# Attention queries of two heads in row halves of the array, denominators on GpSimd, numerators in column halves

## The chip, the core and the metric

The program runs on one core of a Trainium2 chip. The metric is the time of one execution on the device in microseconds (us); a run is compared by its median. The engines are TensorE (PE, matrix products; PEld is its weight load), VectorE (DVE), ScalarE (ACT), GpSimd (POOL) and SyncE (SP, which here issues the DMA transfers). Matrix results land in PSUM, eight banks of 2 KB per partition; everything else lies in SBUF.

## What is computed

A linear attention, then a mixture of four experts, then a gated network; all in 32-bit floating point.

```python
def phi(x):
    proj = np.einsum('bhsd,df->bhsf', x, w_phi)
    proj = proj - np.max(np.abs(proj), axis=-1, keepdims=True)
    return np.concatenate([np.exp(proj), np.exp(-proj)], axis=-1)
q_p, k_p = (phi(q), phi(k))                     # (4, 8, 576, 256)
kv = np.einsum('bhsf,bhsd->bhfd', k_p, v)
z = np.sum(k_p, axis=2)
num = np.einsum('bhsf,bhfd->bhsd', q_p, kv)
den = np.einsum('bhsf,bhf->bhs', q_p, z)[..., None] + 1e-06
x = num / den                                   # as 2304 tokens x 512
...
for e in range(4):
    out += p[:, e:e + 1] * (np.maximum(x @ w1[e], 0.0) @ w2[e])
...
y = (((out @ v1) * (out @ v2)) @ w3) @ w_out
```

## The kernel before

**Recording and order.** The program text does not issue instructions: `op` (L130) and `dma` (L341) record operations with an engine, a guess of their duration, and what they read, write and fill. `Prog.run` (L281) plays the record through a list scheduler with those guesses, once by priority and twice more by due times, and then issues everything in the order that came out. So each engine's queue holds the order that the planner chose, and a changed guess, buffer count or priority moves instructions everywhere. Priorities come from `pg.base`, `KLEAD` and `AHEAD` (how far ahead of the expert work an attention pair is put). In the first 110 us the planner also issues filler products (`spin`, L467, tile `fill_z`) into the gaps that it foresees on TensorE.

**Attention.** Batches and heads are taken as 16 pairs of heads (`p` 0 to 15). `k_side` (L506) projects the keys of both heads, each with its 64 rows in one row half of the array (L540), takes the exponentials, and sums features times values into one PSUM bank `kvp` in column halves (L553); column 64 of the values' tile is a one, so that z falls out as one more column. ScalarE copies the result to `KV`, for pairs 6 to 15 (`SPLIT`) rounded to the one-pass 32-bit format with VectorE's remainder beside it (L591, L594). `q_side` (L605) then works head by head (`h`), half a sequence at a time (`s`, 288 columns): a load of q that brings the 64 rows twice, a rounded copy in the upper rows and the remainder in the lower (L613, L614), two products `Pq` (L623, L624), a copy to SBUF `Ps` (L628), the largest absolute value over the 128 partitions by GpSimd `M` (L631), the subtraction on VectorE (L634), two exponentials into `Eq` (L639). For pairs 6 to 15 `Eq` is split again into a rounded tile and a remainder (L645, L647). The product `num` (L655) has 128 output rows: 64 of the numerator and 64 copies of the denominator; it takes two products in full precision (each stands as two records in the trace), or six of the rounded format for the split pairs. A copy `xq` (L660), a small DMA of the denominator's row to `d9`, a reciprocal, a DMA out and back that spreads it over 64 partitions (`rb`), and one multiplication per head (L680) give the attention output `xr`.

**Experts.** Expert weights come in 16 chunks `c`. Token group 0 (768 tokens) is computed with plain products for the first `KA` = 8 chunks, since these can run while later attention pairs are still at work: per chunk and half group two times twelve products `up` (L800 by `plain_up`), a ReLU on ScalarE and its remainder on VectorE (L855, L857), and three times six products `dn` (L869) that VectorE adds up in `acc` (L890). One half group of one chunk is called a turn below; there are 2 x `KA` = 16. All later chunks and groups use a Strassen scheme (`upa`, `upb`, `upc`, seven times six products in place of eight, by `strassen_up`), with weights prepared by GpSimd (L391, L419). It starts when all of attention is done (`phase_c`) and holds the rest of the program, with `fold` (w3 times w_out, tile `psw`) and the gated network.

**PSUM.** In the attention stage pool `aps` has five banks (`kvp` 1, `kp` 2, `qp` 1, `num` 1) and pool `mma` three, from which `up` and `dn` take turns. Afterwards `mma` keeps its three and `mmb` takes the other five.

Of the kernel before, what the change touches and what calls it, by code (L numbers as in the profile page):

```python
# [308 lines left out]
def fused_kernel(ctx, tc, qT, kT, vt, w_phi, probs, w1, w2, v1, v2, w3T, w_out, out):  # L309
# [196 lines left out]
    def k_side(p):  # L506
# [72 lines left out]
        halves = [
            (lambda t: t()[:, :, 0:4:3], lambda: kvp()[:, :, :, 0:64]),  # L580
            (lambda t: t()[:, :, 1:3], lambda: kvp()[:, :, :, 64:65].to_broadcast([128, 2, 2, 64])),
        ]
        if p not in SPLIT:
            KV = [V("at", [128, 2, 4, 64], F32, "KV0", 2, f"KV{p}")]
            for part, src in halves:
                op(ACT, act(256, False), lambda part=part, src=src: nc.scalar.copy(out=part(KV[0]), in_=src()),
                   reads=[kvp], fills=KV)
        else:
            KV = [V("at", [128, 2, 4, 64], F32R, f"KV{i}", 2 - i, f"KV{i}_{p}") for i in range(2)]
            for part, src in halves:  # L590
                op(ACT, act(256, False), lambda part=part, src=src: nc.scalar.copy(out=part(KV[0]), in_=src()),  # L591
                   reads=[kvp], fills=KV[:1])
            for part, src in halves:
                op(DVE, dve(256), lambda part=part, src=src: nc.vector.tensor_tensor(  # L594
                    out=part(KV[1]), in0=src(), in1=part(KV[0]).bitcast(F32), op=ALU.subtract
                ), reads=[kvp, KV[0]], fills=KV[1:])
# [8 lines left out]
    def q_side(p, KV):  # L605
        b, pr = divmod(p, 4)
        xq = V("at", [128, 2, S], F32, "xq", 2, f"xq{p}")
        d9 = V("at", [128, 2 * S // 128], F32, "d9", 3, f"d9_{p}")
        rd = V("dram", [1, 2 * S], F32, f"rd{p}", 1, f"rd{p}")
        for h in range(2):  # L610
            qr = qr0 if p == h == 0 else load_q(p, h)
            q2 = V("at", [128, S], F32R, "q2", 2, f"q2{p}_{h}")
            op(ACT, act(S), lambda qr=qr, q2=q2: nc.scalar.copy(out=q2(), in_=qr()), reads=[qr], writes=[q2])  # L613
            op(DVE, 786, lambda qr=qr, q2=q2: nc.vector.tensor_tensor(  # L614
                out=q2()[64:128], in0=qr()[64:128], in1=q2()[64:128].bitcast(F32), op=ALU.subtract
            ), reads=[qr], writes=[q2], port=True)
            for s in range(2):
                nm = f"{p}_{h}{s}"
                sl = slice(s * HS, (s + 1) * HS)
                P = V("aps", [128, HS], F32, "num" if p < ALONE and s else "qp", 1, f"Pq{nm}")  # L620

                def proj(P=P, q2=q2, sl=sl):
                    nc.tensor.matmul(P(), wst(), q2()[:, sl], start=True, stop=False)  # L623
                    nc.tensor.matmul(P(), wlo(), q2()[:, sl], start=False, stop=True)  # L624
# [512 lines left out]
```

## Time and profile before

| | |
|---|---|
| median of 3 runs | 1261.15 us (1260.68 to 1261.97) |
| the profiled execution | 1263.01 us, of which the traced span is 1261.2 us |
| busy share of the span | PE 99%, PEld 89%, DVE 74%, ACT 50%, POOL 43% |
| chain that ended last | PE 90%, DVE 5%, DMA 2%, ACT 2% |
| granted TensorE clock | full in nearly every slice |
| first `up` product | 84.7 us after the start |
| first `upa` product (Strassen) | 294.9 us after the start |

The busy time of TensorE is the union of pipelined products, so that a stretch at 100% may still hold waits; what a product takes is read from the distance between starts. The three stretches that the two starts in the table cut out are called the early stage (0 to 84.7), the mixed stage (84.7 to 294.9: attention pairs between plain turns) and the expert stage (the rest).

### The profile page before, as it was taken

The numbers are of one execution on the slowest core, as the hardware profiler recorded it, in microseconds if no ns is written. First come the engines' busy times: TensorE is split into PE (matmuls) and PEld (weight loads), VectorE is DVE, ScalarE is ACT, GpSimd is POOL, SyncE is SP. The second block draws the span as 40 slices with busy tenths as digits, with TensorE's granted clock in tenths as the row PEclk, the third lists the DMA queues.
The fourth block names the chain that finished last, engine by engine and source line by source line (L and its number), as shares of the span: only waits on it lengthen the run. The fifth ranks groups of instructions, "written<-read, shape, count | busy, mean of one in ns | idle before, by whom it ended". The sixth has DMA issues, their size and how long they took to land.

```text
span 1261.2 us, 19437 instructions
## 1 busy us (share of the span) xinstructions
PE 1247.6 (99%) x7449; PEld 1125.8 (89%) x7449; DVE 934.2 (74%) x1446; ACT 628.4 (50%) x1231; POOL 546.9 (43%) x374
## 2 busy tenths in 40 slices
PE   8999999999999999999999999999999999999998
PEld 7779988899999999988889888898899999999997
DVE  6698999979787885587687785698998647634454
ACT  7888888745433333344434343454445545443321
POOL 3432323316333333054544455466676677435220
PEclk9999999999999999999999999999999999999999
DMA  5654454222333321023535432143332212211002
GB/s 173 176 183 130 146 176 140 79 88 84 109 110 109 109 92 43 19 87 121 163 121 176 145 131 83 52 134 115 123 100 78 79 51 84 84 34 51 1 1 100
DMA packets 53197, 128.55 MB, mean 102 GB/s; under 512 B 10352, under 2 KB 14832, under 8 KB 53104
## 3 DMA queue, kind: packets, MB, share of 16 engines
q1 hardware_dynamic: 53104, 127.32, 31.5%
q8 instruction: 58, 0.95, 0.3%
q14 instruction: 35, 0.29, 0.1%
HBM read 109.84 MB, written 17.38 MB: 101 GB/s over the span
## 4 chain that ended last, share of the span: by engine, by line
PE 90%; DVE 5%; DMA 2%; ACT 2%; issue 1%; SPq 0%; DVEq 0%; ACTq 0%
PE dn L869 38%; PE upa L800 13%; PE upb L800 7%; PE up L800 4%; PE psw L940 3%; PE upc L800 3%; PE num L655 3%; PE kvp L553 1%; PE upa_4a L800 1%; PE upa_3b L800 1%; PE upa_3a L800 1%; PE upa_5b L800 1%; PE upa_5a L800 1%; PE upa_4b L800 1%; DVE xr L680 1%
## 5 line engine op out<-in xcount | busy, mean ns | idle before, releaser
L869 PE MATMUL dn<-w_b,h 128*128 128x512 f32 x1728 | 423.7, 391 | 0.0
L869 PEld LDWEIGHTS dn<-w_b,h 128*128 128x128 f32 x1728 | 320.7, 188 | 57.5 <-DVE acc L890 0.3
L391 POOL TENSOR_TENSOR w_a<-raw_a,w_a 128x768 fp32r<-128x768 f32 (+2 forms) x80 | 165.5, 2069 | 227.5 <-ACT w_a L389 202.1
L890 DVE SCALAR_TENSOR_TENSOR acc<-dn,pn,acc 128x512 f32<-128x512 f32 x270 | 200.3, 745 | 54.5 <-PE dn L869 52.6
L391 POOL TENSOR_TENSOR w_b<-raw_b,w_b 128x1024 fp32r<-128x1024 f32 x48 | 122.7, 2555 | 228.3 <-ACT w_b L389 223.2
L631 POOL PARTITION_ALL_REDUCE M<-Ps x64 | 86.4, 1361 | 169.5 <-ACT Ps L628 135.0
L800 PE MATMUL upa<-x_T,w_a 128*128 128x384 f32 x720 | 146.2, 337 | 0.0
L800 PEld LDWEIGHTS upa<-x_T,w_a 128*128 128x128 f32 x720 | 128.5, 187 | 7.2 <-ACT s L823 0.7
L823 ACT COPY s<-upa 128x384 f32<-128x384 f32 x120 | 57.5, 479 | 121.2 <-PE upa L800 120.9
L419 POOL TENSOR_TENSOR raw_a<-raw_a 128x256 f32<-128x256 f32 x128 | 109.8, 858 | 18.3 <-DVE acc L890 6.2
L389 ACT CAST w_b<-raw_b 128x1024 fp32r<-128x1024 f32 x61 | 64.3, 1054 | 103.4 <-PE dn L869 62.7
L869 PE MATMUL dn<-w_b,g 128*128 128x512 f32 x432 | 105.7, 390 | 0.0
L389 ACT CAST w_a<-raw_a 128x1024 fp32r<-128x1024 f32 (+2 forms) x93 | 84.5, 908 | 41.1 <-PE upb L800 16.6
L869 PEld LDWEIGHTS dn<-w_b,g 128*128 128x128 f32 x432 | 80.5, 188 | 13.7
L800 PE MATMUL up<-x_B,w_a 128*128 128x384 f32 x384 | 72.2, 338 | 0.0
L655 PE MATMUL num<-Eq,KV 128*128 128x288 f32 x336 | 67.4, 334 | 3.3 <-ACT xq L660 1.8
L800 PEld LDWEIGHTS up<-x_B,w_a 128*128 128x128 f32 x384 | 66.2, 188 | 1.0
L655 PEld LDWEIGHTS num<-Eq,KV 128*128 128x128 f32 x336 | 51.8, 188 | 10.9 <-ACT xq L660 3.8
L639 ACT ACTIVATE Eq<-Ps 128x288 f32<-128x288 f32 x128 | 51.5, 458 | 15.7 <-DVE Ps L634 15.4
L920 DVE TENSOR_TENSOR oacc<-dn,oacc 128x512 f32<-128x512 f32 x54 | 36.8, 687 | 19.0 <-PE dn L869 18.8
L800 PE MATMUL upa<-x_B,w_a 128*128 128x384 f32 x240 | 49.1, 339 | 0.0
L800 PE MATMUL upb<-x_B,w_a 128*128 128x384 f32 x240 | 49.0, 339 | 0.0
(213 smaller groups left out, 2241.7 us busy)
## 6 DMA issues: line engine op xcount, KB each, us to landing
raw_a<-w SPq DMA_DIRECT2D x37, 512.0 KB, 3.4
raw_b<-w SPq DMA_DIRECT2D x37, 512.0 KB, 3.7
qr<-qT SPq DMA_DIRECT2D x32, 288.0 KB, 3.2
near<-w3T SPq DMA_DIRECT2D x16, 512.0 KB, 4.2
raw_b<-near_wo SPq DMA_DIRECT2D x16, 512.0 KB, 4.3
near<-v SPq DMA_DIRECT2D x16, 512.0 KB, 4.8
vx<-vt SPq DMA_DIRECT2D x16, 330.0 KB, 4.3
kr<-kT SPq DMA_DIRECT2D x15, 320.0 KB, 3.9
```

What stands on the lines that cost most here:

```text
L389: lambda: op(ACT, act(n, sbuf), lambda: nc.scalar.copy(out=hi(), in_=raw[1]()), reads=[*raw[:1], *raw[2:]], fills=[w], after=after),
L391: lambda: op(eng, ns, lambda: e.tensor_tensor(out=lo(), in0=raw[1](), in1=hi().bitcast(F32), op=ALU.subtract), reads=[raw[0], w, *raw[2:]] ...
L419: ops.append(lambda to=to, a=a, b=b, how=how: op(POOL, gp(256), lambda: nc.gpsimd.tensor_tensor(out=raw()[:, to], in0=raw()[:, a], in1=raw ...
L631: op(POOL, 1300, lambda M=M, Ps=Ps: nc.gpsimd.partition_all_reduce(M(), Ps(), channels=128, reduce_op=bass_isa.ReduceOp.absmax), reads=[Ps ...
L639: op(ACT, act(HS), lambda a=a, E=E, Ps=Ps: nc.scalar.activation(out=E()[:, a], in_=Ps(), func=AF.Exp, scale=1.0 - 2 * a), reads=[Ps], fill ...
L655: nc.tensor.matmul(num(), KV[i]()[:, a, 2 * h:2 * h + 2].rearrange("p c d -> p (c d)"), EE[j]()[:, a], start=n == 0, stop=n == len(parts) - 1)
L800: nc.tensor.matmul(ps(), w()[:, a, i, kk * 128:kk * 128 + 128], x()[:, j, kk], start=first and n == 0, stop=last and n == total - 1, skip_ ...
L823: op(ACT, act(TB, False), lambda: nc.scalar.copy(out=t(), in_=ps()), reads=[ps], writes=[t], after=start["C"])
L869: nc.tensor.matmul(ps(), hs[fc]()[:, x, t * 128:(t + 1) * 128], w()[:, fc * 2:fc * 2 + 2, y], start=fc == 0 and n == 0, stop=fc == 1 and n ...
L890: op(DVE, dve(DM) + 61, lambda a=a, ps=ps, share=share: nc.vector.scalar_tensor_tensor(out=a(), in0=ps(), scalar=share(), in1=a(), op0=ALU ...
L920: op(DVE, dve(DM), lambda a=a, ps=ps: nc.vector.tensor_tensor(out=a(), in0=ps(), in1=a(), op=ALU.add), reads=[ps], writes=[a])
L940: nc.tensor.matmul(ps(), wa[v]()[:, k, a, f * 128:f * 128 + 128], wb[v]()[:, 2 * k:2 * k + 2, b], start=g == 0 and k == 0 and n == 0, stop ...
```

## The change

- q of both heads of a pair is loaded once, one head in each row half. `Pq` is then six products (three for each head) on row halves, the two heads' one after the other; pair 0 (`EXACT`) takes q and w_phi in full precision without a split.
- `KV` is one copy in full precision for all pairs; `SPLIT` and the split of `Eq` are gone. Pairs 0 to 4 (below `ALONE` = 5) multiply in full precision with 128 output rows as before. From pair 5 on, the numerators of both heads are formed in column halves of one product tile, and the denominators elsewhere: VectorE weights `Eq` by z (`W`, two instructions), GpSimd adds over the partitions.
- `xq` of pairs 5 to 15 holds both heads on 128 partitions, so that one multiplication gives `xr`.
- `KA` is 7 in place of 8 and `EB` 4 in place of 5: 14 turns, and one Strassen visit more for group 0; two folds move before the last visit of the first kind. `AHEAD` is scaled down.
- Pool `mma` has two banks in place of three (`qp` has two in place of one); after attention a pool `mmx` adds the third again.

```diff
-KA = 8
-EB = 5
-SPLIT = (6, 7, 8, 9, 10, 11, 12, 13, 14, 15)
+KA = 7
+EB = 4
+ALONE = 5
+MORE = 3
+EXACT = (0,)
+QBUFS = 2
-COLUMNS = 130.0
-ALONE = 3
+COLUMNS = 120.0
-AHEAD = (0.05, 0.6, 1.5, 2.4, 2.9, 4.5, 5.5, 6.5, 7.5, 8.5, 9.5, 10.5)
+AHEAD = (0.04, 0.48, 1.2, 1.92, 2.32, 3.6, 4.4, 5.2, 6.0, 6.2, 7.0, 7.8)
-NEAR = (24, 8, 0)
+NEAR = (40 - 2 * (16 - KA), 8, 0)
...
-    pools["mma"] = ec(tc.tile_pool(name="mma", bufs=3, space=PSUM))
+    pools["mma"] = ec(tc.tile_pool(name="mma", bufs=2, space=PSUM))
...
+        KV = V("at", [128, 2, 2, 66], F32, "KV", 2, f"KV{p}")
+        op(ACT, act(264, False), lambda: nc.scalar.copy(out=KV(), in_=kvp()), reads=[kvp], writes=[KV])
         return KV
...
+        qr = load_q(p) if p else qr0
+        rows = [slice(h * 64, h * 64 + 64) for h in range(2)]
+        if p in EXACT:
+            terms = [(lambda: wphi(), lambda: qr())]
+            used = [qr, wphi]
+        else:
+            q2 = V("at", [128, 2, S], F32R, "q2", QBUFS, f"q2{p}")
+            op(ACT, act(S), lambda: nc.scalar.copy(out=q2()[:, 0], in_=qr()), reads=[qr], writes=[q2])
+            op(DVE, dve(S), lambda: nc.vector.tensor_tensor(
+                out=q2()[:, 1], in0=qr(), in1=q2()[:, 0].bitcast(F32), op=ALU.subtract
             ), reads=[qr], writes=[q2], port=True)
+            terms = [(lambda i=i: (wst, wlo)[i](), lambda j=j: q2()[:, j]) for i, j in PASSES]
+            used = [q2, wst, wlo]
+        for s in range(2):
+            sl = slice(s * HS, (s + 1) * HS)
+            Pq = [V("aps", [128, HS], F32, "qp", 2, f"Pq{p}_{h}{s}") for h in range(2)]
+
+            def proj(Pq=Pq, sl=sl):
+                for x, (a, q) in enumerate(terms):
+                    for h in range(2):
+                        nc.tensor.matmul(Pq[h](), a()[rows[h]], q()[rows[h], sl], start=x == 0, stop=x == len(terms) - 1,
+                                         skip_group_check=True)
+
+            op(PE, 915 if len(terms) == 1 else 600, proj, reads=used, writes=Pq)
...
+                W = V("at", [128, HS], F32, "W", 2, f"W{nm}")
+                op(DVE, 280, lambda W=W, E=E, h=h: nc.vector.tensor_scalar(
+                    out=W(), in0=E()[:, 0], scalar1=KV()[:, 0, h, ones[h]:ones[h] + 1], scalar2=None, op0=ALU.mult
+                ), reads=[E, KV], writes=[W], port=True)
+                op(DVE, dve(HS) + 61, lambda W=W, E=E, h=h: nc.vector.scalar_tensor_tensor(
+                    out=W(), in0=E()[:, 1], scalar=KV()[:, 1, h, ones[h]:ones[h] + 1], in1=W(), op0=ALU.mult, op1=ALU.add
+                ), reads=[E, KV], writes=[W], port=True)
+                op(POOL, 1300, lambda W=W, h=h, sl=sl: nc.gpsimd.partition_all_reduce(
+                    D()[:, sl] if h else xq()[:, 1, sl], W(), channels=128, reduce_op=bass_isa.ReduceOp.add
+                ), reads=[W], fills=[D if h else xq], port=600)
+            if p >= ALONE:
+                num = V("aps", [128, HS], F32, "num", 1, f"num{p}_{s}")
+
+                def product(num=num, Es=Es):
+                    for a in range(2):
+                        for h, E in enumerate(Es):
+                            nc.tensor.matmul(
+                                num()[h * 64:h * 64 + 64], KV()[:, a, h, 2 * h:2 * h + 64], E()[:, a], start=a == 0, stop=a == 1,
+                                skip_group_check=True,
+                            )
+
+                op(PE, 1390, product, reads=[KV, *Es], writes=[num])
+                op(ACT, act(HS, False), lambda num=num, sl=sl: nc.scalar.copy(out=xq()[:, 0, sl], in_=num()),
+                   reads=[num], fills=[xq])
...
-            for h in range(2):
+            for h in range(2) if p < ALONE else (0,):
+                half = slice(h * 64, h * 64 + 64) if p < ALONE else slice(0, 128)
...
+    folds = deque(("fold", n, (), None) for n in range(16))
+    for c in range(KA, NE * NQ):
+        if c >= NE * NQ - (8 - KA):
+            visits += [folds.popleft(), folds.popleft()]
+        visits.append(("expert", c, (1, 0), None))
...
+        if late:
+            banks[0] += 1
+            pool = ("mma", "mma", "mmx")[banks[0] % 3]
```

The order moves with it. On TensorE, around the first turn of the second half group (tile names: `num_HS` is head and half, `Pq_HS` likewise, `x_B` the tokens of a plain turn), before:

```order
L800 MATMUL up_10_2233<-x_B_1444,w_a_1936 128x384 x6
L800 MATMUL up_10_2233<-x_B_1882,w_a_1936 128x384 x6
L655 MATMUL num_00_2256<-Eq_9_00_2121,KV_9_2211 128x288
L655 MATMUL num_00_2256<-Eq_9_00_2161,KV_9_2211 128x288
L655 MATMUL num_00_2256<-Eq_9_00_2121,KV_9_2226 128x288
L655 MATMUL num_00_2256<-Eq_9_00_2121,KV_9_2211 128x288
L655 MATMUL num_00_2256<-Eq_9_00_2161,KV_9_2211 128x288
L655 MATMUL num_00_2256<-Eq_9_00_2121,KV_9_2226 128x288
L623 MATMUL Pq_00_2268<-q_0_2087,wst 128x288
L624 MATMUL Pq_00_2268<-q_0_2087,wlo 128x288
L800 MATMUL up_11_2272<-x_B_1444,w_a_1936 128x384 x6
```

and in the change:

```order
L828 MATMUL up_10_2060<-x_B_1473,w_a_1793 128x384 x6
L828 MATMUL up_10_2060<-x_B_1852,w_a_1793 128x384 x6
L670 MATMUL num_1_2087<-Eq_01_2044,KV_2011 64x288
L670 MATMUL num_1_2087<-Eq_11_2058,KV_2011 64x288
L670 MATMUL num_1_2087<-Eq_01_2044,KV_2011 64x288
L670 MATMUL num_1_2087<-Eq_11_2058,KV_2011 64x288
L619 MATMUL Pq_01_2101<-q_1736,wst 128x288
L619 MATMUL Pq_11_2103<-q_1736,wst 128x288
L619 MATMUL Pq_01_2101<-q_1736,wst 128x288
L619 MATMUL Pq_11_2103<-q_1736,wst 128x288
L619 MATMUL Pq_01_2101<-q_1736,wlo 128x288
L619 MATMUL Pq_11_2103<-q_1736,wlo 128x288
```

Where six full-array products of one head and one half and two of `Pq` stood, there are now four in column halves for both heads and six in row halves for both heads; the array goes from full to column halves to row halves to full, where it stayed full before. Over the whole order the array's division changes 98 times before and 155 times in the change, 52 and 96 of them from the first `up` to the first `upa`.

On GpSimd, at pairs 6 and 7, before (`M` is the largest absolute value):

```order
L631 ISA M_00_1261<-Ps_00_1256 128x288
L631 ISA M_01_1322<-Ps_01_1318 128x288
L631 ISA M_10_1394<-Ps_10_1388 128x288
L631 ISA M_11_1438<-Ps_11_1434 128x288
L631 ISA M_00_1601<-Ps_00_1596 128x288
```

and in the change:

```order
L630 ISA M_00_1423<-Ps_00_1412 128x288
L630 ISA M_10_1443<-Ps_10_1421 128x288
L661 ISA xq_1408<-W_00_1433 128x288
L661 ISA D_1491<-W_10_1441 128x288
L630 ISA M_01_1536<-Ps_01_1518 128x288
L630 ISA M_11_1560<-Ps_11_1532 128x288
L661 ISA xq_1408<-W_01_1530 128x288
L661 ISA D_1491<-W_11_1534 128x288
L630 ISA M_00_1629<-Ps_00_1622 128x288
```

Two sums over `W` now stand between the maxima of one half and those of the next, so that a next maximum waits behind two sums, and these wait for VectorE's `W`.

## Rows read from the trace of the kernel before

**Rows 1.** The page: busy time, share of the span and instructions by engine.

```profile
PE 1247.6 (99%) x7449; PEld 1125.8 (89%) x7449; DVE 934.2 (74%) x1446; ACT 628.4 (50%) x1231; POOL 546.9 (43%) x374
```

**Rows 2.** Windows of the stages: length, busy us by engine, clock, DMA.

```profile
0.00:84.70 84.70, 77.69 (x872) 62.55 (x872) 60.73 (x120) 67.54 (x178) 33.64 (x31) 1.00 0.61 181
84.70:294.90 210.20, 207.31 (x1708) 187.56 (x1707) 193.18 (x334) 160.43 (x362) 63.17 (x46) 1.00 0.39 122
...
294.90:1261.20 966.30, 962.62 (x4874) 875.65 (x4872) 680.31 (x995) 400.41 (x691) 450.05 (x298) 1.00 0.28 91
```

**Rows 3.** Timeline, TensorE, mixed stage: start us, length us, records.

```profile
226.73 0.96 PE L655 MATMUL num<-Eq,KV 128*128 128x288 f32 x6
227.53 0.30 PE L623 MATMUL Pq<-q,wst 128*128 128x288 f32 x1
...
227.79 1.55 PE L869 MATMUL dn<-w_b,h 128*128 128x512 f32 x6
```

**Rows 4.** Timeline, TensorE, early stage: `num` in full precision.

```profile
20.11 2.21 PE L655 MATMUL num<-Eq,KV 128*128 128x288 f32 x8
```

**Rows 5.** The same, later, four records.

```profile
71.13 1.24 PE L655 MATMUL num<-Eq,KV 128*128 128x288 f32 x4
```

**Rows 6.** Timeline, TensorE, mixed stage: column halves, row halves and their neighbours.

```profile
233.67 0.96 PE L655 MATMUL num<-Eq,KV 128*128 128x288 f32 x6
234.56 1.15 PE L553 MATMUL kvp<-vx,E 128*64 128x66 f32 x32
235.64 0.40 PE L623 MATMUL Pq<-q,wst 128*128 128x288 f32 x1
...
238.26 1.16 PE L540 MATMUL P<-wphi,kr 64*128 64x128 f32 x16
239.35 2.35 PE L800 MATMUL up<-x_B,w_a 128*128 128x384 f32 x12
241.54 0.42 PE L655 MATMUL num<-Eq,KV 128*128 128x288 f32 x2
```

**Rows 7.** Groups on VectorE, mixed stage: busy us, mean ns, idle before.

```profile
L647 DVE TENSOR_TENSOR Eq<-Eq,Eq 128x576 fp32r<-128x576 f32 x40 | 30.9, 773 | 1.4 <-ACT Eq L645 1.3
L890 DVE SCALAR_TENSOR_TENSOR acc<-dn,pn,acc 128x512 f32<-128x512 f32 x36 | 26.5, 741 | 3.0 <-PE dn L869 2.9
...
L614 DVE TENSOR_TENSOR q<-qr,q 64x576 fp32r<-64x576 f32 x18 | 14.0, 779 | 1.5 <-ACT q L613 1.0
L391 DVE TENSOR_TENSOR w_a<-raw_a,w_a 128x1024 fp32r<-128x1024 f32 x11 | 14.0, 1269 | 0.8 <-ACT w_a L389 0.7
...
L680 DVE TENSOR_TENSOR xr<-xq,rb 64x384 f32<-64x384 f32 x16 | 9.8, 615 | 3.7 <-DMA rb<-rd 3.5
L594 DVE TENSOR_TENSOR KV<-kvp,KV 128x256 fp32r<-128x256 f32 x20 | 7.5, 416 | 0.1
```

**Rows 8.** Groups on VectorE, whole span, nearest to the two `W` instructions.

```profile
L440 DVE SCALAR_TENSOR_TENSOR near<-near 128x512 int32<-128x512 int32 x40 | 28.2, 704 | 0.5
...
L437 DVE TENSOR_SCALAR near<-near 128x512 int32<-128x512 int32 x40 | 25.8, 644 | 21.2 <-ACT near L434 21.2
```

**Rows 9.** Groups on GpSimd, mixed stage.

```profile
L631 POOL PARTITION_ALL_REDUCE M<-Ps x39 | 53.4, 1373 | 120.7 <-ACT Ps L628 95.5 <-DVE x_B L391 10.4 <-DVE q L614 6.6
```

**Rows 10.** Timeline, two VectorE instructions of one kind, the second beside GpSimd's maximum.

```profile
28.97 0.76 DVE L614 TENSOR_TENSOR q<-qr,q 64x576 fp32r<-64x576 f32 x1
...
64.06 1.24 POOL L631 PARTITION_ALL_REDUCE M<-Ps  x1 [1.18 <-ACT Ps L628]
...
64.34 1.06 DVE L614 TENSOR_TENSOR q<-qr,q 64x576 fp32r<-64x576 f32 x1
```

**Rows 11.** Timeline, mixed stage: an `up` and the `acc` that frees a bank.

```profile
138.93 2.25 PE L800 MATMUL up<-x_B,w_a 128*128 128x384 f32 x12
...
139.97 0.75 DVE L890 SCALAR_TENSOR_TENSOR acc<-dn,pn,acc 128x512 f32<-128x512 f32 x1
```

**Rows 12.** Groups on ScalarE, early stage.

```profile
L613 ACT CAST q<-qr 128x576 fp32r<-128x576 f32 x15 | 10.3, 694 | 5.4 <-DMA qr<-qT 4.6 <-PE Pq L624 0.8
```

More of the change, by code (lines that the diff above doesn't have):

```diff
@@ L530, in group @@
         def group(t0, nt):
-            where = ("mma", "mm", 3) if not p and t0 == 2 else ("aps", "kp", 2)
+            where = ("mma", "mm", 2) if not p and t0 == 2 else ("aps", "kp", 2)
             P = [V(where[0], [128, nt, FEAT], F32, *where[1:], f"P{p}_{t0}{h}") for h in range(2)]
@@ L577, in k_side, with load_q @@
             group(t0, nt) if t0 < 4 else rest()
[L579 to L596, printed above, removed]
+        KV = V("at", [128, 2, 2, 66], F32, "KV", 2, f"KV{p}")
+        op(ACT, act(264, False), lambda: nc.scalar.copy(out=KV(), in_=kvp()), reads=[kvp], writes=[KV])
         return KV
-    def load_q(p, h):
+    def load_q(p):
         b, pr = divmod(p, 4)
-        qr = V("at", [128, S], F32, "qr", 3, f"qr{p}_{h}")
-        dma(lambda: nc.sync.dma_start(out=qr(), in_=qT[b, pr, h]), 312000, writes=[qr])
+        qr = V("at", [128, S], F32, "qr", 2, f"qr{p}")
+        dma(lambda: nc.sync.dma_start(out=qr(), in_=qT[b, pr]), 312000, writes=[qr])
         return qr
@@ L606, in q_side @@
         b, pr = divmod(p, 4)
+        ones = (64, 1)
         xq = V("at", [128, 2, S], F32, "xq", 2, f"xq{p}")
-        d9 = V("at", [128, 2 * S // 128], F32, "d9", 3, f"d9_{p}")
+        D = V("at", [128, S], F32, "D", 2, f"D{p}") if p >= ALONE else None
+        d9 = V("at", [128, 2 * S // 128], F32, "d9", 2, f"d9_{p}")
         rd = V("dram", [1, 2 * S], F32, f"rd{p}", 1, f"rd{p}")
-        for h in range(2):
[L611 to L615, printed above, removed]
-            ), reads=[qr], writes=[q2], port=True)
-            for s in range(2):
-                nm = f"{p}_{h}{s}"
[L619 to L624, printed above, removed]
-                op(PE, 2 * mm(HS), proj, reads=[q2, wst, wlo], writes=[P])
@@ L650, in q_side @@
-                num = V(*(("mma", [128, HS], F32, "mm", 3) if p < ALONE else ("aps", [128, HS], F32, "num", 1)), f"num{nm}")
-                parts = [(a, i, j) for a in range(2) for i, j in (PASSES if len(EE) == 2 else PASSES[:1])]
-                def product(num=num, parts=parts, EE=EE, h=h):
-                    for n, (a, i, j) in enumerate(parts):
-                        nc.tensor.matmul(
-                            num(), KV[i]()[:, a, 2 * h:2 * h + 2].rearrange("p c d -> p (c d)"), EE[j]()[:, a], start=n == 0, stop=n == len(parts) - 1
-                        )
@@ L863, in down @@
     def down(w, hs, t, nm):
-        ps = bank(DM, f"dn{nm}")
+        ps = bank(DM, f"dn{nm}", late=visits[int(nm.split("_")[0])][0] != "plain")
         def run():
```

80 lines of the change are left out of this document (42 added, 38 removed).

## The prediction

> **What bounds the kernel now.** I read the page first. TensorE is busy for 99% of the span and no other engine for more than 74% [rows 1], and the granted clock is full in all three stages [rows 2]. So the time follows TensorE's work, as far as the other engines keep up. The windows say where they might not. In the expert stage TensorE has 962.6 of 966.3 us and VectorE 680.3: pure TensorE. In the mixed stage TensorE has 207.3 of 210.2, but VectorE 193.2, which is 92% and the only place where a second engine is near its limit. In the early stage no engine is full: TensorE 77.7 of 84.7 with its fillers, ScalarE 67.5, VectorE 60.7 [rows 2]. There the length comes from the chain through all engines, and TensorE's work counts little.
>
> A product's price is the distance between starts. Six products of the rounded format of 288 columns run from 226.73 to 227.53, 0.133 us each, and two `Pq` from 227.53 to 227.79, 0.13 each [rows 3]. In full precision eight records take 2.21 us and four 1.24 [rows 4, 5]: 0.97 for four more, 0.2425 a record, and two records make a product: 0.485.
>
> Half arrays: 32 records of 66 columns in column halves would take 32 x 0.2425 x 66/288 = 1.78 us one after another and 0.89 two at a time. They run from 234.56 to 235.64, 1.08 [rows 6]. So two run at a time, and 0.19 is lost at the edges. The six products ahead take 0.89 instead of 0.80, 0.09 more on the way in: 0.28 in all. For row halves, 16 records of 128 columns: 1.72 alone, 0.86 in pairs, and 1.09 from 238.26 to 239.35 [rows 6], 0.23 lost, with the way in 0.32. A change of the array's division thus costs about 0.15 us.
>
> **The change, part by part.** *Numerators.* Removed: 10 split pairs x 4 pieces x 6 x 0.133 = 31.9, and pair 5's 4 x 2 x 0.485 = 3.9. Added: 11 pairs x 2 halves x 4 products, two at a time, 22 x 2 x 0.485 = 21.3. Pairs 0 to 4 stay. Gain 14.5 us. No row shows column halves with two different moving tiles, since `kvp` streams the same one to both. Bounds: 21.3 if they overlap as in `kvp`, 42.7 if they don't. I take the first, because `kvp` is the same form and precision.
>
> The Trainium skill (TensorE: Matmul & The Clock Gate, Measured speedup vs the span model) gives 2.38 times for three column tiles. Two tiles at that efficiency would give 1.59, an estimate from that page, and the sum would be 5.6 us worse, 1255.6. `kvp` shows 1.78/1.08 = 1.65 with its edges and 2 without; I go by the row, where the edges are priced apart.
>
> *Projections.* Before, 39 of the 64 pieces (25 maxima stand in the early stage, 39 in the mixed [rows 9]) lie in the mixed stage: 39 x 2 x 0.13 = 10.1. In the changed order 19 of 32 halves lie there, with three products a head, two heads at a time: 19 x 3 x 0.13 = 7.4. Gain 2.7.
>
> *Divisions of the array.* 52 changes become 96 in the mixed stage: 44 x 0.15 = 6.6 lost. They are fewer than the 80 that 40 new groups would make, as many stand beside a `kvp` or `P` of the same division.
>
> *One chunk more in Strassen.* 48 `up` become 42: 6 x (241.54 - 239.35)/12 = 1.1 gained [rows 6]. The `dn` stay. The work of two turns moves to the expert stage, which is full in either case; the folds only move.
>
> *Two banks for `up` and `dn`.* In the mixed stage 73 tiles follow one another in three banks. I compared the start of each with the moment at which the tile two places earlier is free: 13 start before it, by 10.3 us in all. The clearest is the `up` at 138.93, while the `acc` two tiles earlier ends at 139.97 + 0.75 = 140.72, 1.8 us later [rows 11]. So the cost lies between 0 (the new order evicts in time, with VectorE less loaded) and 10.3. I take 2.5, a quarter, since VectorE's load falls.
>
> *Early stage.* Fillers fall from 113 to 91 and ScalarE loses eight of 15 casts of q, 5.6 us at 0.694 [rows 12], part of a chain that isn't ScalarE's alone. Bounds: 0, and 84.7 x 61.9/67.5 = 77.7 if ScalarE set it, a gain of 7. I take 2. Sixteen loads of q less, at a DMA share of 0.61 and 0.39 [rows 2], gain nothing by themselves: TensorE waits for none of them but the first.
>
> *VectorE, mixed stage.* Away: the `Eq` split 30.9, the `KV` split 7.5, nine of 18 q remainders 7.0, some 18 of the `xr` multiplications at 0.615, 11.1, six `acc` of two turns 4.4, and four weight splits 5.1 [rows 7]. To come: 44 times a TENSOR_SCALAR and a SCALAR_TENSOR_TENSOR of 288 columns, by the nearest rows [rows 8] at 288/512 of 644 and 704 ns, 0.36 + 0.40: 33.4. So 193.2 - 66.0 + 33.4 = 161. The stage itself becomes 210.2 - 14.5 - 2.7 + 6.6 + 2.5 less two turns (24 `up` at 0.18 and 18 `dn` at 0.133 x 512/288 = 0.236, 8.6 each), 185 us. VectorE is then at 87%, below today's 92%: hidden. ScalarE only loses work. `W` waits for the second exponential, and behind it in VectorE's queue stand the next `Ps` and the `acc` that frees a bank; that wait is priced with the banks, above.
>
> *GpSimd.* 44 sums at 1.37 are 60 us more on 63.2 [rows 2, 9], 123 of 185: hidden, with a limit. Its queue is in order: the next maximum stands behind two sums, and these behind VectorE's `W`; eight reductions a pair are 11 us, a pair's share of the stage 18. In the expert stage it prepares one Strassen chunk more, at 450 of 966 us [rows 2].
>
> **The sum:** -14.5 - 2.7 + 6.6 - 1.1 + 2.5 - 2 = -11.2. The profiled span is 1261.2 (its execution 1263.01, 1.9 above the median of 1261.15). From the median: **1250.0 us**.
>
> **Rivals.** *A, slower: the column halves don't overlap.* Different moving tiles would then go one after another, and 44 pairs of products cost 0.485 more each, +21.3: 1271. It decides from about 0.25 us lost a pair on. For it: the one row of column halves has a common moving tile. Against: row halves overlap fully with different ones [rows 6].
>
> *B, VectorE and GpSimd get in each other's way.* The same q remainder took 0.76 us alone and 1.06 when it began 0.28 after a maximum [rows 10]. If each new sum stretches one or two VectorE instructions by 0.30, that is 13 to 26 us: 174 to 187 busy of 185. At the 92% that VectorE reaches today the stage lasts up to 187/0.92 = 203, and at 180 it lasts 196, 11 more than in my sum: about 1260, at worst 1268. For it: the nearness to full. Against: the maxima are in today's mean durations already, and many VectorE instructions read PSUM. The Trainium skill (GPSIMD Engine Reference, Key points) says that GpSimd shares its SBUF interfaces with VectorE and contends with instructions that have two SBUF inputs, as the second half of each `W` has. By that rule B is the outcome; the trace agrees for one kind of instruction.
>
> *C, the two banks stall TensorE as often as today's evictions would:* 10.3 instead of 2.5, 1257.8. For it: VectorE's queue stays in order and full of attention work. Against: the order was made for two banks.
>
> *D, the early stage shrinks with ScalarE:* 7 instead of 2, and the mixed stage's 2.9 idle us go, as a numerator no longer waits for a split: 1242.
>
> **Chances.** Forecast 0.46, A 0.08, B 0.20, C 0.12, D 0.14. About 0.2% (2.5 us) is what a measurement here can tell from no change: faster is below 1258.6, slower above 1263.7. Faster: the forecast, D, some two thirds of C and two fifths of B, 0.77. Slower: A and a third of B, 0.14. Same: 0.09. The range takes D, C and B's middle: 1240 to 1262.
>
> **What would show it.** Right: the last attention product to the first `upa` as close as today, a first `upa` near 268 us, an expert stage near 982 (966.3, two turns' work in Strassen form, and no new idle time), four `num` column records of a half in about 1.3 us with the edges, and VectorE near 87% between. Wrong: `num` pairs a full record apart (A); `Ps` or `W` of 0.6 us and more, and TensorE waiting for `Eq` in the mixed stage (B); `dn` or `up` waiting for `acc` or `h` (C); a first `up` well before 82 (D).

## The result, and the profile after

The changed kernel takes **1270.99 us** (median of 4 runs, 1270.49 to 1273.52), the kernel before 1261.56 beside it (1260.68 to 1263.26): a ratio of 1.0077, 95% interval 1.0059 to 1.0095. It is slower by 9.4 us where 11.2 less were forecast. The profiled execution took 1273.52 us, its span is 1271.7.

The page's busy line of the changed kernel answers to [rows 1]: GpSimd has risen from 43% to 52%, TensorE has fallen to 98%.

```profile
PE 1246.9 (98%) x7401; PEld 1098.9 (86%) x7401; DVE 939.4 (74%) x1437; ACT 584.5 (46%) x1138; POOL 655.5 (52%) x425
```

The windows of its three stages (first `up` at 77.4 us, first `upa` at 287.1) answer to [rows 2]:

```profile
0.00:77.40 77.40, 74.12 (x852) 56.98 (x852) 52.53 (x112) 60.22 (x161) 30.98 (x30) 1.00 0.54 160
77.40:287.10 209.70, 192.56 (x1590) 150.08 (x1589) 197.20 (x321) 118.57 (x278) 164.98 (x90) 0.98 0.34 102
287.10:1271.70 984.60, 980.23 (x4963) 891.85 (x4961) 689.71 (x1007) 405.69 (x700) 459.59 (x306) 1.00 0.27 90
```

The early stage is 7.3 us shorter, the expert stage 18.3 longer for its extra chunk (982 was forecast). What went wrong is in the middle: two turns and the split numerators have left the mixed stage, and yet it lasts 209.7 us, 25 more than forecast. TensorE stands idle for 17.1 of them (2.9 before), and VectorE has not become lighter (197.2; 161 was forecast).

Groups of the mixed stage, GpSimd: `M` is the maximum as in [rows 9], the other two are the sums.

```profile
L630 POOL PARTITION_ALL_REDUCE M<-Ps x40 | 56.9, 1464 | 16.0 <-ACT Ps L627 16.0
L661 POOL PARTITION_ALL_REDUCE xq<-W x22 | 52.5, 2387 | 16.4 <-DVE W L658 13.4 <-DMA kr<-kT 2.8
L661 POOL PARTITION_ALL_REDUCE D<-W x22 | 49.9, 2270 | 0.6 <-DVE W L658 0.6
```

A sum takes 2.33 us, not the 1.37 of a maximum: 102.4 us in place of 60. The groups on VectorE answer to [rows 7]:

```profile
L633 DVE TENSOR_TENSOR Ps<-Ps,M 128x288 f32<-128x288 f32 x40 | 28.0, 728 | 1.1 <-POOL M L630 1.1
L658 DVE SCALAR_TENSOR_TENSOR W<-Eq,KV,W 128x288 f32<-128x288 f32 x44 | 24.9, 597 | 0.0
L655 DVE TENSOR_SCALAR W<-Eq,KV 128x288 f32<-128x288 f32 x42 | 24.7, 603 | 5.1 <-POOL xq L661 4.7 <-POOL D L661 0.3
L918 DVE SCALAR_TENSOR_TENSOR acc<-dn,pn,acc 128x512 f32<-128x512 f32 x28 | 20.6, 740 | 1.8 <-PE dn L897 1.7
```

`acc`, which reads a product from PSUM, takes what it took (741 in [rows 7]). The waits of the stage (us in total, times, longest) begin with a chain: the exponential waits for the subtraction, and TensorE's longest waits are for `h` and for a copy that frees the `num` bank.

```profile
ACT Eq L638 <- DVE Ps L633: 33.5, 21, 4.3
...
PE dn L897 <- DVE h L885: 4.4, 5, 1.3
PE num L670 <- ACT xq L676: 3.3, 2, 3.0
...
PE up L828 <- DVE acc L918: 0.9, 2, 0.8
```

One such place in the timeline (start us, length us), with lines of other work left out. The two copies `Ps` are done by 156.21, but their maxima stand behind two sums and run from 158.88 to 161.48. The subtractions stand behind `W` instructions in VectorE's queue as well (0.84 us, and 1.47 for two), and start at 162.23. ScalarE has waited 4.29 us for them, and the next `num` starts 5.84 after the last. At 169.95, with GpSimd idle, a `W` instruction that took 1.35 us beside a sum takes 0.35.

```profile
155.53 0.68 ACT L627 COPY Ps<-Pq 128x288 f32<-128x288 f32 x2
...
156.92 2.05 POOL L661 PARTITION_ALL_REDUCE D<-W  x1
157.05 1.35 DVE L655 TENSOR_SCALAR W<-Eq,KV 128x288 f32<-128x288 f32 x1 [1.00 <-POOL xq L661]
...
158.88 2.60 POOL L630 PARTITION_ALL_REDUCE M<-Ps  x2
159.01 0.84 DVE L655 TENSOR_SCALAR W<-Eq,KV 128x288 f32<-128x288 f32 x1
...
159.75 1.19 PE L670 MATMUL num<-Eq,KV 128*64 128x288 f32 x8
...
160.23 1.47 DVE L658 SCALAR_TENSOR_TENSOR W<-Eq,KV,W 128x288 f32<-128x288 f32 x2
...
160.87 1.67 PE L897 MATMUL dn<-w_b,h 128*128 128x512 f32 x6
...
162.23 1.25 DVE L633 TENSOR_TENSOR Ps<-Ps,M 128x288 f32<-128x288 f32 x2
163.15 1.44 ACT L638 ACTIVATE Eq<-Ps 128x288 f32<-128x288 f32 x4 [4.29 <-DVE Ps L633]
...
165.59 1.19 PE L670 MATMUL num<-Eq,KV 128*64 128x288 f32 x8 [3.05 <-ACT xq L676]
...
169.95 0.35 DVE L655 TENSOR_SCALAR W<-Eq,KV 128x288 f32<-128x288 f32 x1
```

### The profile page after: what moved, and what is told of

Read it like the earlier page. It is cut to its first block, busy times and chain, and to the rows that moved or that the text cites. A ratio compares the mean times of both kernels' runs of the same rounds, so it can differ in the third digit from the quotient of the medians.

```text
span 1271.7 us, 19273 instructions
## 1 busy us (share of the span) xinstructions
PE 1246.9 (98%) x7401; PEld 1098.9 (86%) x7401; DVE 939.4 (74%) x1437; ACT 584.5 (46%) x1138; POOL 655.5 (52%) x425
## 4 chain that ended last, share of the span: by engine, by line
PE 76%; DVE 2%; DMA 1%; ACT 0%; issue 0%; DVEq 0%; ACTq 0%
PE dn L897 35%; PE upa L828 13%; PE upb L828 7%; PE psw L968 3%; PE upc L828 3%; PE upa_4a L828 1%; PE upa_3b L828 1%; PE upa_3a L828 1%; PE upa_5b L828 1%; PE upa_5a L828 1%; PE upa_4b L828 1%; DMA near_v<-near 1%; PE upb_4a L828 1%; PE upb_3a L828 1%; PE upb_3b L828 1%; PE upb_5b L828 1%
## 5 line engine op out<-in xcount | busy, mean ns | idle before, releaser
L395 POOL TENSOR_TENSOR w_a<-raw_a,w_a 128x768 fp32r<-128x768 f32 (+2 forms) x82 | 168.8, 2059 | 225.9 <-ACT w_a L393 202.2
L828 PE MATMUL upa<-x_T,w_a 128*128 128x384 f32 x738 | 149.6, 337 | 0.2 <-ACT s L851 0.2
L828 PEld LDWEIGHTS upa<-x_T,w_a 128*128 128x128 f32 x738 | 131.7, 188 | 7.2 <-ACT s L851 0.6
L423 POOL TENSOR_TENSOR raw_a<-raw_a 128x256 f32<-128x256 f32 x132 | 115.2, 873 | 19.5 <-DVE acc L918 7.0
L638 ACT ACTIVATE Eq<-Ps 128x288 f32<-128x288 f32 x128 | 48.8, 448 | 34.6 <-DVE Ps L633 34.6
L828 PE MATMUL up<-x_B,w_a 128*128 128x384 f32 x336 | 63.6, 341 | 0.9 <-DVE acc L918 0.9
L828 PEld LDWEIGHTS up<-x_B,w_a 128*128 128x128 f32 x336 | 57.9, 188 | 4.1 <-DVE acc L918 2.0
L661 POOL PARTITION_ALL_REDUCE xq<-W x22 | 52.5, 2387 | 16.4 <-DVE W L658 13.4
L661 POOL PARTITION_ALL_REDUCE D<-W x22 | 49.9, 2270 | 0.6 <-DVE W L658 0.6
```

The costliest lines, as they stand in the source:

```text
L395: lambda: op(eng, ns, lambda: e.tensor_tensor(out=lo(), in0=raw[1](), in1=hi().bitcast(F32), op=ALU.subtract), reads=[raw[0], w, *raw[2:]] ...
L423: ops.append(lambda to=to, a=a, b=b, how=how: op(POOL, gp(256), lambda: nc.gpsimd.tensor_tensor(out=raw()[:, to], in0=raw()[:, a], in1=raw ...
L638: op(ACT, act(HS), lambda a=a, E=E, Ps=Ps: nc.scalar.activation(out=E()[:, a], in_=Ps(), func=AF.Exp, scale=1.0 - 2 * a), reads=[Ps], fill ...
L661: op(POOL, 1300, lambda W=W, h=h, sl=sl: nc.gpsimd.partition_all_reduce(D()[:, sl] if h else xq()[:, 1, sl], W(), channels=128, reduce_op= ...
L828: nc.tensor.matmul(ps(), w()[:, a, i, kk * 128:kk * 128 + 128], x()[:, j, kk], start=first and n == 0, stop=last and n == total - 1, skip_ ...
```

## The experiments

Theories: **S**, the sums on GpSimd cost the loss, by how long they hold its queue (S1) or by slowing VectorE while they read (S2); **W**, VectorE is simply too full with `W`; **C**, the two banks; **A**, column halves that don't overlap. A falls by the timeline above: the eight records of `num` at 159.75 are followed by `dn` 1.12 us later, 4 x 0.2425 = 0.97 and an edge of 0.15; one after another they would take 1.94. Of the 22 such groups in the trace, 13 are followed after 1.02 to 1.12 us. C is small by the waits above, 0.9 us, and e2 below, which keeps the two banks, leaves TensorE idle for 1.1 us of its mixed stage.

Most kernels here ran once. Executions of the kernel before lie up to 5 us apart (1260.30 to 1265.61 beside e16), so a difference between two single runs is good to some 3 us, an estimate.

**The sum alone: replaced or left out.** Each is the changed kernel, with the same order of instructions on every engine.

```diff
 e1_absmax
-reduce_op=bass_isa.ReduceOp.add
+reduce_op=bass_isa.ReduceOp.absmax
 e2_no_sum
-nc.gpsimd.partition_all_reduce(D()[:, sl] if h else xq()[:, 1, sl], W(), ...)
+nc.gpsimd.memset(D()[0:1, sl] if h else xq()[0:1, 1, sl], 1.0)
 e7_fill
-nc.gpsimd.partition_all_reduce(...)
+(nc.gpsimd.memset(scratch(), 1.0), nc.gpsimd.memset(scratch(), 1.0), nc.gpsimd.memset(<as e2>))
```

> The GpSimd reduction over W takes the largest absolute value in place of the sum (the denominators are then other numbers); the order of all instructions is that of the changed kernel. Theory Q (the mixed stage is paced by GpSimd's queue, because a sum takes 2.33 us where a maximum takes 1.4): the 44 reductions shrink by 0.9 us each, 40 us of GpSimd time, and the time falls to 1250 to 1258. Theory V (VectorE's own added work, W, fills the stage): no more than 3 us fall, 1268 or above. Theory C (two PSUM banks): no change.

> The 44 GpSimd sums become a fill of one row with ones (denominators are left out); W is still computed on VectorE and the order stays. Theory Q, and also theory X (GpSimd's reductions stretch VectorE's instructions, and stretched they fill the stage): about 1250, with VectorE's Ps subtraction back from 728 ns to about 460 and the first W instruction near 0.36 us. Theory V: above 1262. Theory C: no change from 1271.

> Each sum becomes two fills of a scratch tile of 1024 columns and one of a row: GpSimd is to be held for about as long as by a sum (some 2 us), but reads nothing; denominators are left out; the order stays. Theory Q (occupied queue: the next maximum stands behind 2 x 2.3 us): 1264 or more if the fills come to 2.2 us together. Theory X (the sums' traffic stretches VectorE, and that fills the stage): within 5 us of the run without sums (1244.9), with VectorE's Ps subtraction near that run's 523 ns.

Measured, one run each: e1 **1252.01**, e2 **1244.86** (before beside both: 1261.47), e7 **1254.21** (before 1260.41). The mixed stage of e1, e2 and e7, each with rows of GpSimd or VectorE:

```profile
78.20:265.90 187.70, 184.12 (x1591) 145.96 (x1590) 178.44 (x321) 118.69 (x279) 132.03 (x90) 1.00 0.38 115
L661 POOL PARTITION_ALL_REDUCE xq<-W x22 | 37.2, 1689 | 19.5 <-DVE W L658 16.5 <-DMA kr<-kT 2.8
L661 POOL PARTITION_ALL_REDUCE D<-W x22 | 33.8, 1538 | 0.6 <-DVE W L658 0.6
```

```profile
75.70:258.70 183.00, 181.88 (x1591) 145.78 (x1590) 170.79 (x321) 119.22 (x278) 77.33 (x89) 1.00 0.38 117
258.70:1243.10 984.40, 980.07 (x4963) 891.79 (x4961) 689.97 (x1007) 405.91 (x700) 460.13 (x306) 1.00 0.28 90
...
L658 DVE SCALAR_TENSOR_TENSOR W<-Eq,KV,W 128x288 f32<-128x288 f32 x44 | 24.4, 587 | 0.0
L655 DVE TENSOR_SCALAR W<-Eq,KV 128x288 f32<-128x288 f32 x42 | 21.9, 536 | 0.0
...
L633 DVE TENSOR_TENSOR Ps<-Ps,M 128x288 f32<-128x288 f32 x40 | 17.7, 470 | 0.0
...
142.86 2.59 POOL L630 PARTITION_ALL_REDUCE M<-Ps  x2 [4.37 <-ACT Ps L627]
143.03 0.72 DVE L655 TENSOR_SCALAR W<-Eq,KV 128x288 f32<-128x288 f32 x1
...
146.89 0.81 DVE L633 TENSOR_TENSOR Ps<-Ps,M 128x288 f32<-128x288 f32 x2
...
147.37 1.44 ACT L638 ACTIVATE Eq<-Ps 128x288 f32<-128x288 f32 x4 [0.60 <-DVE Ps L633]
147.65 1.19 PE L670 MATMUL num<-Eq,KV 128*64 128x288 f32 x8
...
150.37 1.19 PE L670 MATMUL num<-Eq,KV 128*64 128x288 f32 x8
...
154.22 0.36 DVE L655 TENSOR_SCALAR W<-Eq,KV 128x288 f32<-128x288 f32 x1
```

```profile
77.40:268.00 190.60, 184.51 (x1592) 146.38 (x1589) 181.95 (x323) 118.38 (x279) 154.51 (x175) 1.00 0.38 113
L663 POOL MEMSET scratch<- 128x1024 f32 x86 | 83.7, 974 | 2.5
...
L657 DVE TENSOR_SCALAR W<-Eq,KV 128x288 f32<-128x288 f32 x42 | 30.3, 736 | 0.0
...
L635 DVE TENSOR_TENSOR Ps<-Ps,M 128x288 f32<-128x288 f32 x40 | 17.2, 464 | 1.1 <-POOL M L632 1.1
```

Without sums everything else of the change gives 1244.9, and 26.1 us lie between that and 1271.0: S holds. The timeline rows of e2 up to 150.37 are the place shown above: the maxima wait for the copies and not for sums, ScalarE waits 0.60 instead of 4.29, and the two `num` stand 2.72 us apart instead of 5.84. Holding the queue as long as a sum does (e7: 2 x 0.974 + 0.36 = 2.31 us a piece) costs 9.4 us; a reduction that also reads over partitions, but shorter (e1: 1.61 us), costs 7.2. Neither is 26. So S1 explains about 9 at most: the fill also slows the first `W` instruction (736 against 536 ns), and VectorE is busy for 182.0 us against 170.8, so that part of the 9 is VectorE's. About 17 more come with what the sum does while it runs.

**VectorE's `W` left out.** W predicts that the loss goes; the sums stay, over `E()[:, 0]`.

```diff
-                W = V("at", [128, HS], F32, "W", 2, f"W{nm}")
-                op(DVE, 280, ... nc.vector.tensor_scalar(out=W(), ...
-                op(DVE, dve(HS) + 61, ... nc.vector.scalar_tensor_tensor(out=W(), ...
```

> W is left out (88 VectorE instructions, 50 us busy in the mixed stage) and GpSimd sums the first exponential itself, so the denominators are other numbers; all sums stay at 2.3 us. Theory Q: GpSimd has as much to do as before, the time stays at 1266 or more. Theory V: 1250 or below. Theory X: VectorE loses 50 of 197 us busy, the time falls to 1250 to 1258.

Measured **1265.24**, one run, in an order of its own: 5.8 of the 26 come back, although VectorE is down to 166 us of a stage of 198. The subtraction takes 908 ns here, and now it waits for the maximum, 10.4 us in all where it waited 1.1 in the changed kernel:

```profile
L633 DVE TENSOR_TENSOR Ps<-Ps,M 128x288 f32<-128x288 f32 x41 | 37.1, 908 | 10.4 <-POOL M L630 10.4
```

So `W` alone isn't the cause, but VectorE's fullness isn't refuted. In the changed kernel VectorE is busy for 94% of the mixed stage (197.2 of 209.7). In e1, e7, e11 and e11c it is 93 to 95%, and the stage's length goes with its busy time, from 178.4 in 187.7 (e1) to 201.4 in 215.2 (e11c); in e2 TensorE itself is full (181.9 of 183.0). This reads as VectorE at its limit, filled by its own stretched instructions. With `W` out of the way the 10.4 us point to GpSimd's queue as the next limit, so that relieving one of the two gives back little.

**The subtraction read from PSUM.** `Ps - M` stands on the chain maximum, subtraction, exponential, `num`. In e11 it takes the projection from PSUM; e11c has the same order of instructions but reads `Ps` from SBUF.

```diff
 e11_psum
-out=Ps(), in0=Ps(), in1=M(), op=ALU.subtract), reads=[M], writes=[Ps], port=True)
+out=Ps(), in0=P(), in1=M(), op=ALU.subtract), reads=[M, P], writes=[Ps])
 e11c_sbuf: as e11, but in0=Ps()
```

> The subtraction of the maximum reads the projection from PSUM in place of the copy in SBUF, so that it has one SBUF input; rows of acc and of the key side (one or no SBUF input) kept their length beside the sums. The PSUM tile is held longer and the planner makes another order, the same as in e11c_sbuf. If the stretched subtraction carries the 17 us: Ps at 450 to 500 ns throughout and 8 to 17 us below e11c_sbuf. If the stretch of W and the weight splits carries them, or GpSimd's queue: within 4 us of e11c_sbuf.

> The control of e11_psum: the same order, the subtraction reads both operands from SBUF as in the changed kernel. Expected at 1268 to 1275, with Ps near 730 ns in the mixed stage.

Measured, one run each: e11 **1271.58**, e11c **1280.46** (before 1263.0). Mixed stage and subtraction of e11, then of e11c:

```profile
78.50:283.50 205.00, 189.57 (x1586) 147.37 (x1585) 191.64 (x322) 121.20 (x286) 158.57 (x93) 0.99 0.34 101
L633 DVE TENSOR_TENSOR Ps<-Pq,M 128x288 f32<-128x288 f32 x44 | 19.2, 443 | 1.6 <-POOL M L630 1.5
```

```profile
77.80:293.00 215.20, 192.48 (x1586) 148.01 (x1585) 201.35 (x322) 121.55 (x286) 161.38 (x93) 0.98 0.33 98
L633 DVE TENSOR_TENSOR Ps<-Ps,M 128x288 f32<-128x288 f32 x44 | 32.4, 741 | 2.7 <-POOL M L630 2.6
```

One operand moved to PSUM: 741 becomes 443 ns, 8.9 us less in an identical order. That is S2, shown for the instruction on the chain. In the changed kernel's order it would be about half of the 17, which is not shown: e11c is itself 9.5 us above the changed kernel. As a repair it fails, since the projection's bank is held longer: TensorE waits 6.3 us for it, and the time equals the changed kernel's.

**Repairs that compute everything.** None beats the kernel before.

```diff
 e4_plan:     the planner's guess for a sum 1300 -> 2350
 e6_act:      e4, and the first W instruction on ScalarE (nc.scalar.mul)
 e8_alone9:   e6, ALONE = 9: 28 sums; pairs 5 to 8 in full precision on the full array
 e9_port:     guess 2050, port=1200;   e9b_port_alone9: e9 and ALONE = 9
 e12_psum_act: e11 with e6;            e13_psum_alone9: e12 and ALONE = 9
 e16_spread:  e8, the seven pairs with sums spread over the stage (5, 7, 9, 10, 12, 14, 15)
```

> Only the planner's guess of a sum changes, 2350 ns in place of 1300; the same instructions in another order. Theory P (the loss comes from an order made for sums of 1.3 us; GpSimd's 165 us busy would fit into a stage of 185): 1256 or less. Theory Q without P (the chain maximum, subtraction, exponentials, W, sum can't be packed closer): within 4 us of 1271.

> As e4_plan, and the first W instruction (603 ns on VectorE in the mixed stage) moves to ScalarE, which is at 57% there. VectorE loses 25 us of 197. Theory X: 6 to 12 us below e4_plan. Theory Q: within 3 us of e4_plan, as the run without W at all gained only 6.

> As e6_act, with ALONE = 9: four pairs fewer take the sums (28 in place of 44), and their numerators go through the whole array in full precision, 4 x 2 halves x (4 x 0.485 - 0.97 - 0.28) = 5.5 us more on TensorE, 37 us less on GpSimd. Theory Q: a gain over e6_act, to about 1256. If TensorE is the bound again in e6_act: 5 us above it.

> Only the planner's two guesses for a sum change: 2050 ns long (1300 before), and VectorE's instructions with SBUF inputs kept off for the first 1200 ns of it (600 before). Theory P' (the order can keep such instructions away from the sums if the planner knows): 1258 or less, Ps back to about 460 ns in most cases. Theory X as it stands (44 x 2.2 us during which VectorE is stretched can't be scheduled around in a stage where it's at 90%): within 5 us of 1271.

> As e9_port with ALONE = 9 (28 sums in place of 44, 5.5 us more on TensorE). Theory X: near 1260, like e8_alone9; ScalarE's part of W in that run would then have been worth nothing. If P' holds: below 1256.

> e11_psum with the first W instruction on ScalarE and 2350 ns told for a sum. If stretched VectorE instructions carry the loss: 2 to 8 us below e11_psum. If GpSimd's queue does: the same as e11_psum.

> e12_psum_act with ALONE = 9 (28 sums). e8_alone9 gave 1259.9 with the subtraction from SBUF; if that is still stretched there by 28 sums, 1252 to 1257, ahead of the kernel before; if TensorE is the bound there already, 1258 to 1261.

> As e8_alone9 (first W instruction on ScalarE, the planner told 2350 ns for a sum, seven pairs with sums, the others on the full array in full precision, everything computed), but the seven pairs are spread over the stage (5, 7, 9, 10, 12, 14, 15) in place of the last seven (9 to 15). Each full-precision half costs TensorE 1.94 us in place of 1.12 to 1.27 and each sum, by the loss of 26 us over 44, some 0.6 us. If the loss grows with how densely the sums stand (queue and shared memory interface): 1252 to 1258, TensorE's idle time in the mixed stage under 4 us. Rival: each sum costs the same wherever it stands: 1258 to 1261, as e8.

| kernel | us | before beside it | ratio, 95% |
|---|---|---|---|
| e4_plan | 1269.69 | 1260.41 | one run |
| e6_act | 1270.57 | 1260.41 | one run |
| e8_alone9 | 1259.88 | 1260.41 | one run |
| e9_port | 1272.83 | 1262.94 | one run |
| e9b_port_alone9 | 1265.96 | 1262.94 | one run |
| e12_psum_act | 1278.21 | 1263.0 | one run |
| e13_psum_alone9 | 1273.4 | 1263.0 | 1.0075 (1.0049 to 1.0102) |
| e16_spread | 1261.51 | 1262.44 | 0.9995 (0.9983 to 1.0006) |

Telling the planner the true length moves nothing, nor does work taken from VectorE: none of these orders hides the sums. Fewer sums help: e8 lies 10.7 us below e6, which brings it level with the kernel before and not ahead, as full-precision products on TensorE take 5.5 us by its expectation's count. Where the sums stand does not matter (e16 as e8). e12 and e13 miss their expectations by far: 6.6 us above e11 and 13.5 above e8, though the subtraction reads PSUM and the first `W` instruction is gone from VectorE. Why, no run here separates; it speaks against taking the stretched instructions for the whole of the loss.

**Denominators on TensorE, with the rest of the change kept.** e10 forms them by four products of 32 columns in column quarters; e14 takes numerators and denominators of pairs 6 to 15 from the kernel before (six split products); e15 has `ALONE = 16`.

```diff
 e10_pe_den
+    k = 32 * (2 * a + h)
+    nc.tensor.matmul(den()[k:k + 32], KV()[:, a, h, ones[h]:ones[h] + 1].to_broadcast([128, 32]), E()[:, a], ...)
 e14_split, e15_alone16
-ALONE = 5
+ALONE = 16
 e14_split
+SPLIT = tuple(range(6, 16))
```

> No W and no sums: TensorE forms the denominators of pairs 5 to 15 itself, four products of 32 columns (z, 32 times) for two heads and two feature halves, in four column groups, 22 times; ScalarE copies them out, two small DMAs more a pair. If four groups run at a time as two do: 22 x (0.485 + 0.15 to 0.30) = 14 to 17 us more on TensorE over the run without sums (1244.9, less up to 3 for VectorE without W): 1256 to 1262. If they go one after another: 22 x 1.94 = 43 us, above 1280. Theory X is supported if the time lies clearly below 1271 with TensorE's idle time in the mixed stage under 4 us.

> The changed kernel's projections in row halves, exact first pair, seven plain chunks and two banks, but numerators and denominators as in the kernel before for pairs 6 to 15 (KV and Eq split, six one-pass products of 288 columns on the full array); no W, no sums; computes the whole reference. If the loss lies in the sums alone, and the rest of the change keeps what it brings: the kernel without sums took 1244.9; 22 halves now cost 12 x 0.133 = 1.60 us in place of four column products of 1.12 to 1.27, some 0.3 to 0.5 each, 7 to 11 us; six array divisions a pair fewer give 3 back: 1249 to 1253, POOL near 65 us busy in the mixed stage and Ps near 0.52 us. VectorE takes the Eq split (30.9 us) in place of W (40), so it stays near 172. Rival: the rest of the change is worth nothing without the cheap numerators: 1258 to 1264, as before.

> The changed kernel with ALONE = 16: all pairs multiply in full precision on the full array with 128 output rows; no W, no sums, no split of Eq; computes the whole reference. Theory: 22 halves cost 2 pieces x 2 products x 0.485 = 1.94 us in place of 1.12 to 1.27, so 15 to 18 us of TensorE's time over the kernel without sums (1244.9), and 3 back for fewer divisions: 1257 to 1260, with VectorE near 130 us busy in the mixed stage. Rival: VectorE and the queue still set the stage, then TensorE's added time fills gaps that stand there anyway, and the time stays at 1250 or below.

Measured: e10 **1268.49**, ratio 1.0042 (1.0026 to 1.0059); e14 **1267.56**, 1.0036 (1.0023 to 1.0050); e15 **1272.16**, 1.0081 (1.0064 to 1.0098). All three miss. The mixed stages of e14 and e15:

```profile
80.20:277.30 197.10, 191.23 (x1643) 167.44 (x1642) 174.09 (x302) 149.27 (x341) 64.30 (x45) 1.00 0.36 107
```

```profile
78.40:279.00 200.60, 195.95 (x1573) 163.25 (x1572) 153.11 (x258) 130.20 (x301) 59.87 (x46) 1.00 0.37 109
```

GpSimd is at ease, and VectorE is busy for 88% and 76%, so these two read mostly TensorE's side. Over their whole spans TensorE is busy for 1249.8 and 1254.9 us against 1234.2 in e2: 15.6 and 20.7 more. By the prediction's price of column halves (0.97 us a half) e14 should add 20 x (1.60 - 0.97) + 2 x (1.94 - 0.97) = 14.5, since pair 5 isn't split there, and e15 22 x (1.94 - 0.97) = 21.3; my expectations had counted the edges in the 1.12 to 1.27 as saved, and by this count they weren't. The other 5 us of each are idle time, mostly `dn` waiting for `h` (5.1 and 4.3 us). So without the cheap numerators the rest of the change, in the order it has here, loses a little (e14), and it can't be kept as a gain.

e10 stands 23.6 us above e2. Its denominators account for 22 x 0.62 = 13.6 of that (rows at the end); the rest stays unexplained. It is the only run here that keeps the cheap numerators and computes everything without sums, and it is no gain either.

**The banks.** e5 gave `up`, `dn` and `num` a common pool of three.

```diff
-    pools["mma"] = ec(tc.tile_pool(name="mma", bufs=2, space=PSUM))
+    pools["mma"] = ec(tc.tile_pool(name="mma", bufs=3, space=PSUM))
-    num = V("aps", [128, HS], F32, "num", 1, f"num{p}_{s}")
+    num = V("mma", [128, HS], F32, "mm", 3, f"num{p}_{s}")
```

> Three banks for up and dn again; the numerator tiles share them in place of a bank of their own. Theory C: the time falls by 8 to 12 us, to about 1261. Theories Q, V and X: within 4 us of 1271.

Measured **1311.02**, one run, and nothing about banks: the planner hands out the tiles of one pool in recorded order, so `num` came before any `up`, and the first `up` stood at 217 us. C is judged by the waits and by e2.

## Why the prediction was wrong

Stage by stage, the forecast, the kernel without sums, and the changed kernel:

| stage | forecast | e2 | changed |
|---|---|---|---|
| early | 82.7 | 75.7 | 77.4 |
| mixed | 185 | 183.0 | 209.7 |
| expert | 982 | 984.4 | 984.6 |

**The step that failed** is "*GpSimd.* 44 sums at 1.37 are 60 us more ... 123 of 185: hidden, with a limit." The price was that of the same instruction with another operator [rows 9], and it had no range, although the trace of before showed no sum. An addition over the partitions took 2.33. And "hidden" was read from a busy share, where the queue serves a chain: a maximum behind two sums is late however idle the engine is on average (158.88 above, where the copies were done at 156.21). e7 puts this at 9.4 us at most. With it fell the step before it, VectorE "at 87%, below today's 92%: hidden": it left out what the sums do to VectorE, which was busy for 94% of the stage.

**Rival B** named the other part, with too low a price and ceiling. It took 0.30 us per stretched instruction, 13 to 26 us of VectorE's time; VectorE did rise by 26.4 from e2 (197.2 - 170.8). Its end, "at worst 1268", allowed VectorE 187 us; 197.2 were measured, which at B's 92% makes 214 us of stage (209.7 measured). B had no place for the chain: one stretched instruction (470 to 728 ns on the mean) stands between maximum and `num`, and e11 against e11c gives 8.9 us for it. A chance of 0.20 and a range that ended at 1262 left this out. The Trainium skill (GPSIMD Engine Reference, Key points) has the contention for VectorE instructions in a 2-port perf mode or with two SBUF inputs. The trace agrees for the subtraction, which has two. The first `W` instruction reads one SBUF tile and a column of scalars, and took 1.35 us beside a sum (timeline above) against 0.35 at 169.95; whether it runs in a 2-port mode no run here shows.

**What held.** *Numerators*: A is refuted, and e14 and e15 differ from e2 by nearly what 0.97 us a half predicts. The Trainium skill (TensorE: Matmul & The Clock Gate, Measured speedup vs the span model) would have given 1.59 for two tiles, the prediction's estimate from that page; the timeline shows 2 apart from the edge. That the changed kernel came out at A's 1271 is a coincidence. *Banks*: 2.5 taken, 0.9 measured. *Chunk*: the expert stage 2 us over. *Early stage*: 2 taken, 9 in e2 and 7.3 in the changed kernel; D had the size, though no run tests its reason, ScalarE. *VectorE*: 161 forecast, 170.8 in e2, since the two `W` instructions take 0.54 and 0.59 even without sums, not 0.36 and 0.40: 12.9 us more by the two rows of e2 against 33.4. The price of the first was right for a GpSimd that stands idle (0.36 at 154.22 in e2) and wrong beside a maximum (0.72 at 143.03). It cost nothing there.

**What stays open.** e7 bounds the queue at 9 of the 26.1 us. e11 against e11c gives 9 for the subtraction, in another order, and net of the 6.3 us of waits for the bank. The remaining 8 are argued only, and the parts may overlap: the other stretched instructions (q's remainder 747 ns in e2, 1058 in the changed kernel), and TensorE's clock. That fell twice in the changed kernel to the lower of its levels, 1.2 GHz (0.50 of full speed in the second row below), after TensorE had waited 2.19 us for a copy of `KV` and, at 165.59 above, 3.05 for the copy of `xq`:

```profile
104.00:120.00 16.00, 13.00 (x126) 9.80 (x124) 15.25 (x26) 9.22 (x24) 13.08 (x8) 0.79 0.30 87
113.00:114.00 1.00, 1.00 (x22) 1.00 (x24) 1.00 (x2) 1.00 (x4) 1.00 (x1) 0.50 0.00 0
160.00:176.00 16.00, 12.95 (x114) 10.06 (x112) 14.86 (x26) 9.42 (x22) 10.28 (x7) 0.89 0.42 126
...
110.58 1.19 PE L670 MATMUL num<-Eq,KV 128*64 128x288 f32 x8 [2.19 <-ACT KV L583]
```

At means of 0.79 and 0.89 over 16 us each that is at most 3.4 + 1.8 = 5.2 us, an estimate; e1, e2 and e7 show 1.00. The clock has a part in the 8.9 us too: by their rows e11c lost some 0.02 x 215.2 = 4.3 us to it and e11 some 0.01 x 205.0 = 2.1, estimates. Why an addition slows VectorE more than a maximum of the same shape (subtraction 728 ns against 555 in e1) no run here tells.
